# Block-sparse attention with a low-rank mixer on one core: casting transfers for half of the attention inputs

## The chip, the cores and the metric

The kernel runs on one core of a Trainium2 chip. The metric is the device time of one execution in microseconds (us), median of the runs. A core has a matrix engine (PE, with its weight loads shown as PEld), a vector engine (DVE), a scalar engine (ACT), GpSimd (POOL), and a queue engine (SP) that only issues transfers. Transfers are issued from SP's or POOL's queue (a few from ACT's) and are carried out by sixteen shared DMA engines. A *casting* transfer changes the type of the numbers as it writes them.

## The reference

Four batches, eight heads, 768 positions, 64 numbers a head. Attention with a mask by blocks of 32 positions (neighbours, first and last block, and three sampled blocks per row), then a mixer: a low-rank mix over positions, and two dense layers with a ReLU between them.

```python
scores = scale * np.matmul(q, k.transpose(0, 1, 3, 2))
scores = np.where(mask, scores, -1000000000.0)
attn = np.exp(scores - max) / (sum + 1e-09)
x = np.matmul(attn, v)                      # heads side by side: [4, 768, 512]
h = x.transpose(0, 2, 1) @ U @ V            # rank 32 over the positions
u = x + h.transpose(0, 2, 1)
out = u + np.maximum(u @ w_ch1, 0.0) @ w_ch2   # 512 -> 2048 -> 512
```

Inputs and outputs are 32-bit floats; the kernel computes its products from 16-bit floats.

## The kernel before

The heads are taken in pairs: 16 pairs, four to a batch (pairs 0 to 3 are batch 0, and so on). T = 6 tiles of 128 positions make up the 768. For a pair the work is: load q, k and v (384 KB each, as floats); cast each to a 16-bit tile; turn q and k so that a head's numbers lie along the partitions; score products on PE; exponentials on ACT; from pair 4 on, a product with the 0/1 mask on DVE (L1016); products with v on PE (L402); division by the row sum on DVE (L532, L539). When a batch's four pairs are done, its rows are mixed (`mix_all`, `mix_parts`), the 16-bit rows `xh` are turned into `uT` by four transposing transfers from SP (L611, `turn`), and the first dense layer starts from `uT` (L673, `w1`), its ReLU being on ACT (L685) or DVE (L687). The second layer follows (L748) with sums of weights and of hidden rows prepared on DVE (L709, L843), and its results are added to the float rows `xf` on DVE (L867, L891), which SP stores (L695, L893). While one batch's pairs run, PE fills up with the dense layers of the batch before. The last batch's layers stand alone at the end.

What the change and the prediction touch:

- `load_qk` (L145) and `load_v` (L158): for pair i, SP issues one transfer for each of q, k and v into a float tile (`ldpool`, two tiles of each kind in turn; rows of 1,536 bytes). Then `cast` (L136) has POOL copy it into the 16-bit tile: `stqld` and `stkld` for q and k (`stpool`, two of each in turn), and a slice of `vts[b % 2]` for v. From pair 6 on a cast is split into four of 128x192 (L142).
- `front(i)` (L373): for pairs 5 to 15, SP issues two transposing transfers (L375) from the 16-bit tiles of pair i to `qpl[i % 2]` and `kpl[i % 2]`. Each waits for the casts of pair i, and until PE is done with the scores of pair i - 2, which used the same target. The scores of these pairs are the products of L1001, in three groups a pair.
- `loads(i)` (L1024): calls `front(i + 1)`, and then the loads of pair i + 2, which `tc.issue_after` places behind that front in the order of issue.
- `load_w1` and `load_w2` (L351, L357): the dense layers' weights. They come by casting transfers that POOL issues straight into 16-bit tiles: four for w1 (128 rows of 8,192 bytes each), four for w2 (512 rows of 2,048 bytes each), the latter made by `hold` (L1036) when pair 4 begins.

The order of work on PE, DVE, ACT and SP is written out by hand: the words of `PLAN` (L436) are taken one after the other, and for instance `L.5` stands for `loads(6)`. POOL's order is not written out; the scheduler of the language sets it from what it reckons to be ready. All waits between engines follow from the tiles that an instruction reads and writes.

Of the kernel before, what the change touches and what calls it, by code (L numbers as in the profile page):

```python
# [13 lines left out]
FP16 = mybir.dt.float16  # L14
# [5 lines left out]
P = 128  # L20
# [3 lines left out]
def kernel(  # L24
# [14 lines left out]
    nc = tc.nc  # L39

    B, H, S, D = q.shape
    BLK = 32
    NB = S // BLK
    T = S // P
    HD = H * D
    HP = H // 2
# [32 lines left out]
    stpool = ctx.enter_context(tc.tile_pool(name="stpool", bufs=2))  # L79
# [34 lines left out]
    vts = [consts.tile([P, H, T, DV], FP16, name=f"vt{i}") for i in range(2)]  # L114
# [19 lines left out]
    sts = {}  # L134

    def cast(i, dst, ld):  # L136

        if i < HP + 2:
            return nc.gpsimd.tensor_copy(out=dst, in_=ld)
        for h in range(2):  # L140
            for ts in (slice(0, T // 2), slice(T // 2, T)):
                last = nc.gpsimd.tensor_copy(out=dst[:, h, ts], in_=ld[:, h, ts])  # L142
        return last

    def load_qk(i):  # L145
        b, hp = divmod(i, HP)
        last = None
        for src, nm in ((q, "qld"), (k, "kld")):
            ld = ldpool.tile([P, 2, T, D], FP32, tag="ld" + nm, name=nm)
            nc.sync.dma_start(  # L150
                out=ld,
                in_=src[b, 2 * hp : 2 * hp + 2].rearrange("h (p t) d -> p h t d", t=T),
            )
            sts[i, nm] = stpool.tile([P, T, 2, D], FP16, tag="st" + nm, name="st" + nm)
            last = cast(i, sts[i, nm].rearrange("p t h d -> p h t d"), ld)
        return last

    def load_v(i):  # L158
        b, hp = divmod(i, HP)
        ld = ldpool.tile([P, 2, T, D], FP32, tag="ldv", name="vld")  # L160
        nc.sync.dma_start(
            out=ld,
            in_=v[b, 2 * hp : 2 * hp + 2].rearrange("h (p t) d -> p h t d", t=T),
        )
        cast(i, vts[b % 2][:, 2 * hp : 2 * hp + 2, :, 0:D], ld)
# [67 lines left out]
    with tc.manual_schedule(  # L233
# [8 lines left out]
            out=sb[0:NB].rearrange("k z r w -> k (z r w)"),  # L242
            in_=sampled_blocks.bitcast(I32)
# [12 lines left out]
        for n in range(2):  # L256
# [3 lines left out]
            out=first, in_=nc.const_aps.tensor(1.0, [P, 1], FP32), func=AF.Exp  # L260
# [22 lines left out]
        def first_row(n, c, copy):  # L283
# [8 lines left out]
            out=neq[0:NB], in0=sb[0:NB, :, :, 0],  # L292
# [3 lines left out]
            out=a01[0:NB], in_=neq[0:NB], axis=mybir.AxisListType.X, op=ALU.min  # L296
        )
        nc.vector.scalar_tensor_tensor(
            out=bias[0:NB, :, 0:NB], in0=a01[0:NB, None].broadcast_to([NB, 2, NB]),
# [21 lines left out]
        for n in range(2):  # L321
            first_cast(1, n, nc.gpsimd.tensor_copy)
        nc.vector.memset(Ut, 0.0)
        load_v(0)
        load_qk(1)
        second_set()
        load_v(1)
        load_mix()

# [21 lines left out]
    def load_w1(cs):  # L351
        for cc in cs:
            nc.gpsimd.dma_start(
                out=w1t[:, cc, :], in_=moe_w_ch1[cc * P : (cc + 1) * P, :]
            )
# [13 lines left out]
    def plain(i):  # L369
        augs[i] = (qpl[i % 2], kpl[i % 2])  # L370
        return augs[i]

    def front(i):  # L373
        for nm, dst in zip(("qld", "kld"), plain(i)):
            last = nc.sync.dma_start_transpose(  # L375
                dst.rearrange("c (t p) -> c t p", t=T),
                sts[i, nm].rearrange("p t h d -> p (t h d)"),
            )
        return last
# [139 lines left out]
    class Pair:  # L519
# [6 lines left out]
        def divide(self, h, pav):  # L526
            head = 2 * self.hp + h
            if h == 0:
                self.xh = xpool.tile([P, T, P], FP16, tag="xh", name="xh", bufs=6)
                self.bt.xh[self.hp] = self.xh  # L530
            rcp = misc.tile([P, T], FP32, tag="rcp", name="rcp")
            nc.vector.reciprocal(out=rcp, in_=pav[:, :, D])  # L532
            xh = self.xh[:, :, h * D : (h + 1) * D]
            xf = self.bt.xf[:, :, head * D : (head + 1) * D]
            late = self.i >= HP + 2
            if late:
                then("y", lambda: nc.scalar.copy(out=xh, in_=xf))
            for dst in (xh, xf)[late:]:
                nc.vector.tensor_tensor(  # L539
                    out=dst, in0=pav[:, :, 0:D],  # L540
                    in1=rcp[:, :, None].broadcast_to([P, T, D]), op=ALU.mult,
                )
            if h and self.i == HP:
                loads(self.i + 1)
# [338 lines left out]
    def down_out(t, k):  # L883
# [17 lines left out]
        "x": lambda i, c: pairs[i].add_part(c), "d": lambda i, c: pairs[i].cast_part(c),  # L901
        "a": lambda b, c, jj, e: relus.pop((b, c, jj))("ba"[e]),
        "T": lambda i: pairs[i].turn(), "L": lambda i: loads(i + 1),
        "Z": lambda b, tau, u: store(b, 2 * tau + u),
        "S": pair_sum, "H": pair_down, "D": pair_out,
# [118 lines left out]
    def loads(i):  # L1024
        behind = ExitStack()
        if HP + 1 < i + 1 < NPAIR:
            behind.enter_context(tc.issue_after(front(i + 1).ins))
        if i + 2 < NPAIR:
            with behind:
                last = load_qk(i + 2)  # L1030
                load_v(i + 2)
            if i == 1:
                with tc.issue_after(last.ins):
                    load_w1(range(NCC))
# [10 lines left out]
    def begin(i):  # L1045
        if i and i % HP == 0:
            bts[i // HP] = Batch()
        pairs[i] = Pair(i, bts[i // HP])
        if i == HP:
            front(HP + 1)  # L1050
        elif i == HP + 2:
            for c in range(1, 4):
                nc.sync.dma_start(out=Vt[c * R : (c + 1) * R], in_=Vt[0:R])
        for m in {0: (0,), 1: (1, 2), 3: (3,), 4: (4,)}.get(i, ()):
            loads(m)
        if i == HP:
            hold(kpl[1])
# [105 lines left out]
```

## Time and profile before

| | |
|---|---|
| Median of 3 runs | 273.36 us (273.31 to 276.48) |
| Span of the profiled execution, first to last instruction | 271.1 us |
| Median over that span, for what lies around it | 2.3 us |
| Granted PE clock, mean over the span | 0.997 |
| POOL's casts of pairs 8 to 15 | 96, from 80.4 to 185.9 us |
| POOL's casts of pair 7 | end at 75.5 us |
| q transfer from SP, issue to landing, median | 3.5 us |
| k transfer, the same | 5.3 us |
| v transfer, the same | 4.6 us |
| Transposing transfer, issue to landing, median | 2.8 us |

Of the profiled execution only the span is given, not a time of its own; the table sets the median of the runs beside it. The profile's page gives each engine's busy time, and in 40 slices of the span (6.8 us each) the busy share in tenths, 9 being 90% or more. The view of waits sums the time that an engine stood idle before an instruction, by what ended it (total us, times, longest us). The view of a line gives its instructions' shortest, median and longest duration in ns and their first and last start in us. In the order of time a row is a start and a length in us.

### The profile page before, as it was taken

The page shows a single profiled execution, that of the slowest core. Times are in us where ns is not written, and L with a number is a line of the kernel's source. Part 1 is how long each engine was busy: PE and PEld are TensorE (multiplying, and loading weights), DVE is VectorE, ACT ScalarE, POOL GpSimd, SP SyncE. Part 2 cuts the span into 40 slices and gives each one's busy share as a digit, 9 for nine tenths or more (in the row PEclk, how much of TensorE's full clock was granted, in tenths as well). Part 3 has the DMA queues.
Part 4 walks back from the last instruction along what each step waited for, and adds up shares of the span by engine and source line. Part 5 has one row for each costly group of instructions (what it writes and reads, how often), then busy time and mean ns, then how long its engine had stood idle before and what let it go on. Part 6 is the DMA issues. An engine that isn't in the chain of part 4 may idle for free.

```text
span 271.1 us, 7373 instructions
## 1 busy us (share of the span) xinstructions
PE 261.9 (97%) x3008; PEld 182.1 (67%) x3008; DVE 235.3 (87%) x475; ACT 202.5 (75%) x264; POOL 84.7 (31%) x164
## 2 busy tenths in 40 slices
PE   7899999999999999999999999999999999999993
PEld 3577776555567778565666877565667788657882
DVE  5699988988999998868688997688998999999992
ACT  3889998897989666788888847788997943889100
POOL 4479104931628643035624660044000000000000
PEclk9999999999999999999999999999999999999998
DMA  5799997999974664872527356670200116300024
GB/s 161 239 305 316 199 210 173 225 131 198 155 222 67 201 204 91 278 217 59 178 45 190 64 212 117 221 208 16 46 0 2 41 41 142 134 0 0 22 78 136
DMA packets 49698, 37.58 MB, mean 139 GB/s; under 512 B 30528, under 2 KB 46816, under 8 KB 49664
## 3 DMA queue, kind: packets, MB, share of 16 engines
q1 hardware_dynamic: 46688, 32.67, 45.9%
q0 software_dynamic: 2688, 4.19, 10.9%
q8 instruction: 23, 0.38, 0.6%
q10 hardware_dynamic: 288, 0.24, 0.3%
q14 instruction: 11, 0.09, 0.1%
HBM read 27.67 MB, written 6.29 MB: 125 GB/s over the span
## 4 chain that ended last, share of the span: by engine, by line
PE 72%; DVE 17%; DMA 4%; ACT 2%; issue 1%; SPq 1%; POOL 0%; DVEq 0%; ACTq 0%
PE ps L748 28%; PE ps L673 20%; PE ps L402 9%; PE ps L1001 8%; DVE est L1016 5%; DMA qld<-in_q_dram 3%; PE ps L951 2%; DVE xf L867 2%; DVE xf L539 2%; DVE sums L843 1%; DVE res L709 1%; DMA vld<-in_v_dram 1%; ACT est L1010 1%; PE ps L970 1%; DVE sums L709 1%
## 5 line engine op out<-in xcount | busy, mean ns | idle before, releaser
L1010 ACT ACTIVATE est<-ps 128x1536 f16<-128x1536 f32 x72 | 100.6, 1450 | 18.9 <-PE ps L1001 18.9
L673 PE MATMUL ps<-uT,w1t 128*128 128x384 f16 x384 | 70.2, 326 | 0.2 <-DVE hid L687 0.2
L1016 DVE TENSOR_TENSOR est<-est,mask 128x1440 f16<-128x1440 f16 x72 | 65.5, 933 | 0.2
L673 PEld LDWEIGHTS <-w1t 128*128 128x128 f16 x384 | 35.6, 98 | 26.9 <-issue 7.0
L402 PEld LDWEIGHTS <-est 128*128 128x128 f16 x1152 | 40.2, 97 | 7.2 <-ACT hid L685 1.3
L402 PE MATMUL ps<-vt,est 128*128 128x65 f16 x1152 | 43.3, 193 | 0.1
L142 POOL CAST stqld<-qld 128x192 f16<-128x192 f32 x40 | 19.9, 540 | 73.2 <-DMA qld<-in_q_dram 36.0
L748 PEld LDWEIGHTS <-hid 128*128 128x128 f16 x360 | 34.3, 98 | 7.0 <-issue 1.9
L685 ACT ACTIVATE hid<-ps 128x384 f16<-128x384 f32 x63 | 29.7, 495 | 4.7 <-PE ps L673 4.3
L1001 PE MATMUL ps<-qpl,kpl 64*128 64x512 f16 (+1 forms) x288 | 31.6, 325 | 0.0
L748 PE MATMUL ps<-w2t,hid 128*128 128x256 f16 x240 | 31.3, 273 | 0.2 <-DVE xf L539 0.2
L867 DVE TENSOR_TENSOR xf<-xf,ps 128x256 f32<-128x256 f32 x63 | 25.0, 411 | 3.7 <-PE ps L748 3.3
L687 DVE TENSOR_SCALAR hid<-ps 128x384 f16<-128x384 f32 x33 | 18.2, 553 | 8.1 <-PE ps L673 7.5
L748 PEld LDWEIGHTS <-sums 128*128 128x128 f16 x216 | 20.3, 98 | 4.7 <-issue 1.1
L142 POOL CAST stkld<-kld 128x192 f16<-128x192 f32 x40 | 22.3, 597 | 2.5 <-DMA kld<-in_k_dram 2.5
L960 ACT ACTIVATE est<-ps 128x768 f16<-128x768 f32 x30 | 22.5, 813 | 0.6 <-PE ps L951 0.6
L1001 PEld LDWEIGHTS <-kpl 64*128 64x128 f16 x288 | 12.1, 94 | 14.3 <-issue 9.1
L748 PE MATMUL ps<-res,sums 128*128 128x256 f16 x144 | 19.4, 273 | 0.3 <-DVE xf L867 0.3
L622 ACT CAST xh<-xf 128x384 f16<-128x384 f32 x24 | 11.0, 510 | 10.4 <-DVE xf L618 10.4
L539 DVE TENSOR_TENSOR xf<-ps,rcp 128x384 f32<-128x384 f32 x32 | 17.7, 553 | 0.8
L142 POOL CAST vt<-vld 128x192 f16<-128x192 f32 x40 | 17.9, 487 | 0.0
L748 PE MATMUL ps<-res,hid 128*128 128x256 f16 x120 | 15.9, 273 | 0.0
(121 smaller groups left out, 341.5 us busy)
## 6 DMA issues: line engine op xcount, KB each, us to landing
vld<-in_v_dram SPq DMA_DIRECT2D x16, 384.0 KB, 4.6
qld<-in_q_dram SPq DMA_DIRECT2D x15, 384.0 KB, 3.5
kld<-in_k_dram SPq DMA_DIRECT2D x15, 384.0 KB, 5.5
out_dram<-xf SPq DMA_DIRECT2D x18, 256.0 KB, 2.2
w1t<-in_moe_w_ch_dram POOLq DMA_DIRECT2D x4, 512.0 KB, 8.2
w2t<-in_moe_w_ch_dram POOLq DMA_DIRECT2D x4, 512.0 KB, 10.4
out_dram<-xf SPq DMA_DIRECT2D x12, 128.0 KB, 1.7
qld<-in_q_dram SPq DMA_DIRECT2D x2, 192.0 KB
```

What stands on the lines that cost most here:

```text
L142: last = nc.gpsimd.tensor_copy(out=dst[:, h, ts], in_=ld[:, h, ts])
L402: nc.tensor.matmul(pav[:, sc, :], est[:, n, sc * P : (sc + 1) * P], vts[b % 2][:, 2 * hp + h, g, 0 : D + 1], start=(g == 0 and sc == 0), s ...
L539: nc.vector.tensor_tensor(out=dst, in0=pav[:, :, 0:D], in1=rcp[:, :, None].broadcast_to([P, T, D]), op=ALU.mult,)
L673: nc.tensor.matmul(pt, w1t[:, cc, jj * P : (jj + 1) * P], bts[b].uT[:, cc, c * HS : (c + 1) * HS], start=(cc == 0), stop=(cc == NCC - 1), ...
L685: nc.scalar.activation(out=dst, in_=pt, func=AF.Relu)
L687: nc.vector.tensor_scalar_max(out=dst, in0=pt, scalar1=0.0)
L748: nc.tensor.matmul(acc[key], lhsT, rhs, start=(first and i == 0), stop=(i == len(pairs_) - 1), skip_group_check=True,)
L867: nc.vector.tensor_add(out=x, in0=x, in1=acc[a, b, tau])
L960: lambda: nc.scalar.activation(out=dst, in_=ps, func=AF.Exp, scale=0.125),
L1001: nc.tensor.matmul(units[h][:, u * S + lo : u * S + hi], kT[drows[h], g * P : (g + 1) * P], qT[drows[h], lo:hi], start=True, stop=True, sk ...
L1010: nc.scalar.activation(out=both[h], in_=units[h].rearrange("p (g n) -> p g n", g=2), func=AF.Exp, scale=0.125,)
L1016: lambda: nc.vector.tensor_mul(out=masked(both[h]), in0=masked(both[h]), in1=masked(mask[:, 2 * j : 2 * j + 2, :]),),
```

## The change

For pairs 8 to 15 (batches 2 and 3) `load_qk` and `load_v` call a new function, `load_cast`, in which POOL issues casting transfers from the float inputs straight into the 16-bit tiles: one for each head of each of q, k and v, so six a pair, each of 768 rows of 64 numbers (256 bytes read, 128 written). The float tiles, SP's three transfers and POOL's twelve casts of such a pair are gone. The loads of these pairs are no longer placed behind the front of the pair before. Pairs 0 to 7 are unchanged.

```diff
+    DIRECT = 2 * HP
+
+    def load_cast(i, src, dst):
+
+        b, hp = divmod(i, HP)
+        for h in range(2):
+            nc.gpsimd.dma_start(
+                out=dst[:, h],
+                in_=src[b, 2 * hp + h].rearrange("(p t) d -> p t d", t=T),
+            )
+
     def load_qk(i):
         b, hp = divmod(i, HP)
         last = None
+        if i >= DIRECT:
+            for src, nm in ((q, "qld"), (k, "kld")):
+                sts[i, nm] = stpool.tile([P, T, 2, D], FP16, tag="st" + nm, name="st" + nm)
+                load_cast(i, src, sts[i, nm].rearrange("p t h d -> p h t d"))
+            return
...
     def load_v(i):
         b, hp = divmod(i, HP)
+        if i >= DIRECT:
+            load_cast(i, v, vts[b % 2][:, 2 * hp : 2 * hp + 2, :, 0:D])
+            return
...
         if HP + 1 < i + 1 < NPAIR:
-            behind.enter_context(tc.issue_after(front(i + 1).ins))
+            turned = front(i + 1)
+            if i + 2 < DIRECT:
+                behind.enter_context(tc.issue_after(turned.ins))
```

## The prediction

> **What bounds the kernel now.** I read the page's busy table and its 40 slices first, then the costliest groups and the waits, then the order of time of each queue that the change touches.
>
> ```profile
> PE 261.9 (97%) x3008; PEld 182.1 (67%) x3008; DVE 235.3 (87%) x475; ACT 202.5 (75%) x264; POOL 84.7 (31%) x164
> PE   7899999999999999999999999999999999999993
> POOL 4479104931628643035624660044000000000000
> DMA  5799997999974664872527356670200116300024
> ```
>
> PE is at 9 in every slice from the third to the last but one. POOL works only until two thirds of the span, and the sixteen DMA engines are about half used from slice 12 (81 us) to 28. POOL's casts of the last eight head pairs (8 to 15) lie between 80.4 and 185.9 us; that is where the change acts. So I asked what PE waits for from 76 to 190 us:
>
> ```profile
> PE ps L748 <- DVE xf L867: 0.3, 2, 0.2
> PE ps L653 <- DVE a L643: 0.2, 1, 0.2
> PE ps L748 <- DVE xf L539: 0.2, 1, 0.2
> ```
>
> In 114 us PE stands for 0.7 us, and never for a load. This is the most that a faster DVE or an earlier load can give back. The chain of waits puts DVE beside PE on the path (17%, against 72%), but there DVE and PE are both full: 19.76 and 19.52 us busy of the 20 us from 80 to 100.
>
> Then the product with the mask (L1016) on DVE, from 80 to 100 us with casts beside it, and from 186 to 215 us with none (columns: shortest, median, longest ns, first and last start):
>
> ```profile
> L1016 DVE TENSOR_TENSOR est<-est,mask x6: 894/984/1042, 83.7 to 92.0; 128x1440 f16<-128x1440 f16 x6
> L1016 DVE TENSOR_TENSOR est<-est,mask x15: 897/900/910, 185.9 to 214.8; 128x1440 f16<-128x1440 f16 x15
> ```
>
> A cast on POOL costs such a product up to 0.14 us. Last, what limits the new transfers: on SP, the last of the four turns of batch 1's tokens,
>
> ```profile
> 107.28 1.24 SPq L611 DMA_TRANSPOSE uT<-xh  x1
> ```
>
> PE's first use of it in the order of time,
>
> ```profile
> 110.18 0.82 PE L673 MATMUL ps<-uT,w1t 128*128 128x384 f16 x4
> ```
>
> and the issues that POOL makes already, with the DMA queues of the page (packets, MB, share of 16 engines):
>
> ```profile
> L359 POOL DMA_DIRECT2D w2t<-in_moe_w_ch_dram x4: 742/748/761, 48.1 to 55.8; - x4
> ```
>
> ```profile
> q1 hardware_dynamic: 46688, 32.67, 45.9%
> q0 software_dynamic: 2688, 4.19, 10.9%
> ```
>
> These turns land 2.7 to 2.8 us after their issue, so at 110.0 us, and PE comes for the result at 110.18. Batch 2 is alike: issue at 167.22, landing at 170.0, use at 170.25. Two spare gaps of 0.2 us are the tightest places near a DMA that I found.
>
> **The casts that go.** POOL loses 96 casts of 128x192 (0.35 us each when undisturbed, 0.34 to 1.06 in fact). None is on the path: front(8) on SP waits for its cast until 82.6 and 84.9 us, lands by 87.7, and the first scores of pair 8 run at 93.03; later pairs have more. What the casts cost is the collisions with DVE. I took each DVE operation from 80 to 190 us against the fast tenth of its own kind: the excess is 1.4 us (80 to 100), 1.4 (100 to 145), 0.9 (145 to 164) and 0.4 (164 to 190), 4.1 us together. PE can turn only its own 0.7 us of waiting into time. Bounds: 0 and 0.7 us; I take 0.5: the waits stand at 95, 99, 152 and 160 us, in or just behind stretches with casts.
>
> **The transfers that come.** Per pair 6 transfers from POOL take the place of 3 from SP. POOL's own time for one: w1's four transfers (128 rows each) took 0.54 to 0.67 us and w2's four (512 rows) 0.74 to 0.76. A new one has 768 rows; by the slope between those groups that is about 0.85 us, so 5.1 us a pair, against 4.0 to 7.6 us of casts now. Bounds: 0.54 us, and 1.1 if all of w2's 0.75 grew with the rows. The closest pairs follow each other after 12.3 us (first scores at 165.81 and 178.12), so POOL's time is hidden even at 1.1. DVE should not feel an issue: a mask product at 56.09, beside w2's issues (55.03 to 56.51), took 0.90 us, the undisturbed value.
>
> DMA time: the trace's packet records show, for transfers of POOL with a cast, 96 ns for 2,048 bytes read and 324 for 8,192 (medians), a straight line of 20 ns plus 0.037 ns a byte. A new packet (256 bytes read, 128 written) is then 30 ns. Bounds: 18 ns, the 256-byte packets of the transposes, and 96 ns, the cheapest cast packet seen. 768 packets on 16 engines are 48 each, 1.4 us a transfer and 8.6 us a pair, against 3.1 us now (48 packets of 65 ns). It is hidden while a load lands in time: the first needs come 4 us before a pair's first scores (turn 1.3 to issue, 2.8 to land).
>
> **What moves.** Loads of pair i+2 no longer stand on SP behind front(i+1); on POOL they wait only until front(i) has read the tile, as two tiles rotate. SP loses 1.5 us of issues a pair; front, the turns and the stores behind them come no later by it. On POOL the new issues are queued behind the casts of pair 7, which end at 75.5 us, or, if the scheduler puts them first, ahead of them from 56.7 on, when front(6) has landed. Pair 10's loads then follow front(8), pair 11's front(9) (after 88.8, when pair 7's last scores free the target), pair 12's front(10) (117.4), pair 15's front(13) (about 157). A POOL issue that waits holds only other loads behind it, and in one order pair 7's casts, whose front lands 3.5 us before its use. Value products now wait for the v transfer itself; they run after the pair's first scores, later than q and k are needed.
>
> **New collisions.** The turns of uT share the engines with loads. Before 100.8 us pair 11's loads should be nearly drained (issued at about 92 to 98, 8.6 us of data), and pair 12's wait until 117; pair 15's run from 155 to about 165 and meet the first two of four turns at 162.9. The slowest transpose of the trace, kpl's at 140.67 with loads issued right behind it, landed after 3.8 us and not 2.8: so the bound is 1.0 us at each of two places, less 0.2 us to spare, 1.6 us together; the lower bound is 0. I take 0.2, since the last turn, which counts, is clear of loads in both.
>
> Sum against this execution: span 271.1 - 0.5 + 0.2 = 270.8 us. The median of the three runs is 273.36, 2.3 us above the span for what lies around it; so I forecast 273.1 us. Own range: 273.4 - 0.7 to 273.4 + 1.6, 272.7 to 275.0.
>
> The trace holds no 128-byte write with a cast. Its 256-byte packets, the transposes', at 18 ns lie on the line of the larger plain ones (65 ns for 1,536 bytes, 84 for 2,048), so they show no surcharge for being small, and by them the sum stays 273.1. A page speaks against the change: the Trainium skill, "DMA: Bandwidth & Descriptors", section Specifications, has line rate begin at 512 bytes, with the engine reading, modifying and writing below that. It gives no price; by it the time would be that of rival 1.
>
> **Rivals.** (1) *The small packets make the DMA engines the bound.* Pair 15's q and k must land by about 199 us, and from 75.5 us on that leaves 123.5. Transposes (24 of 0.9 us) and stores (12 of 0.7) take 30, which leaves 93 us for 46 transfers: 2.0 us each, 42 ns a packet. Above that point it decides. At 50 ns the 46 take 110 us, 17 us too many: 290 us. At 96 ns it would be 119 us more. For it: 30 ns is stretched eightfold beyond the smallest cast packet seen, and small writes were not seen. Against it: the straight line, and the transposes' 18 ns. Chance 0.09.
>
> (2) *A wait moves into POOL's order.* POOL's order is the scheduler's: in the trace w2's issues stand between casts. If pair 8's six stood ahead of w2's last two, these would leave at 62 us and not at 55, and land some 8.6 us late, at 81 and not 72.7; DVE takes that part at 75.24. That is 6 us: 279 us. Against it: the w2 issues are made earlier in the program and are ready before front(6) lands. Chance 0.07.
>
> (3) *DVE's relief is worth all it measures*, 4.1 us: 269.3 us. For it: the chain is DVE's from 77 to 95 us. Against it: PE's idle time. Chance 0.04. That the transfers would not cast is no case here, as w1 and w2 are loaded so.
>
> **Chances.** Forecast 0.80, rivals 0.09, 0.07 and 0.04. About 2% (5.5 us) is what a measurement of this kernel can tell from no change. Faster by more needs over 5.5 us, which no case holds; 0.02 for what I missed. Slower takes (1) and most of (2): 0.14. Same: 0.84. The range takes the forecast's own with some room toward (2) and (3), and leaves out 0.18: 271.5 to 276.5.
>
> **What would show it.** Right: mask products at 0.90 us throughout from 80 to 190; POOL issues near 0.85 us; packets of 128 bytes near 30 ns; PE without a new wait at L673 after the turns. Wrong: PE waiting at L1001 for a front that waits for a load (rival 1), DVE at L709 waiting for w2 near 75 us (rival 2), transposes landing after 3.8 us or more, or POOL issues of 2 us.

## The result and the profile after

The changed kernel takes 273.55 us (median of 22 executions, 271.24 to 277.66) against 273.58 us of the kernel before (22 executions, 272.94 to 276.48). The ratio is 0.9939, with a 95% interval of 0.9911 to 0.9967; ratios leave out executions far above the fastest of their kernel, here the six highest of the change's 22 (275.76 us and up) and none of before's. The ratio of the medians of all executions is 1.000. The same kernel, measured once more beside the experiments, gave 274.08 us (272.14 to 278.75) and a ratio of 0.9994 (0.996 to 1.0028), or 1.002 by the medians. So the change is worth between nothing and six parts in a thousand, and the changed kernel reaches higher times than any of before's.

The first profile of the changed kernel is of an execution of 275.82 us (span 274.0 us), so the profile after is that of the second measurement: 272.87 us, span 271.1 us. Its page:

```profile
PE 262.0 (97%) x3008; PEld 182.4 (67%) x3008; DVE 233.9 (86%) x475; ACT 202.4 (75%) x264; POOL 74.9 (28%) x116
PE   7899999989999999999999999999999999999994
POOL 4488602792597670040404040000000000000000
DMA  6699999999999999894918696620200116400024
q0 software_dynamic: 40320, 8.92, 38.2%
q1 hardware_dynamic: 40160, 23.23, 35.8%
```

PE has the same sum, but not the same places: there is an 8 in the ninth slice (54 to 61 us), ahead of the stretch that the change acts on. DVE has lost 1.4 us. POOL is at 9 from 54 to 61 us and from 75 to 81, where it was at 3 and 2. In the queues, POOL's packets have gone from 2,688 to 40,320, and their share from 10.9% to 38.2%.

The mask products from 80 to 100 us (shortest, median, longest ns):

```profile
L1035 DVE TENSOR_TENSOR est<-est,mask x7: 895/901/910, 80.3 to 93.4; 128x1440 f16<-128x1440 f16 x7
```

None is longer than 0.91 us, where before the median was 0.98. What PE waited for from 78 to 215 us is down to one line:

```profile
PE ps L1020 <- DMA kpl<-stkld: 0.4, 1, 0.4
```

It is new: scores waiting for a turn of k, at 81 us. Ahead of that, from 50 to 78 us, PE has one wait, which explains the 8 in the ninth slice:

```profile
PE ps L1020 <- DVE hid L706: 0.9, 1, 0.9
```

It ends at 58.77 us. DVE comes late there because one mask product just before took twice its time, beside POOL's casts of pair 6:

```profile
56.34 1.91 DVE L1035 TENSOR_TENSOR est<-est,mask 128x1440 f16<-128x1440 f16 x1
56.86 1.89 POOL L142 CAST vt<-vld 128x192 f16<-128x192 f32 x4
```

The new issues on POOL, by tile:

```profile
L151 POOL DMA_DIRECT2D vt<-in_v_dram x16: 821/821/955, 15.7 to 100.5; - x16
L151 POOL DMA_DIRECT2D stqld<-in_q_dram x16: 821/821/821, 70.7 to 156.8; - x16
L151 POOL DMA_DIRECT2D stkld<-in_k_dram x16: 818/821/830, 78.2 to 158.4; - x16
```

An issue takes 0.821 us. The columns to look at are the first and last starts: q and k run from 70.7 to 158.4 us, as the prediction had it, but v begins at 15.7 us, for pairs whose scores come at 94 us and later.

To see where time went in and out of the executions, the start of each pair's first scores (L1001 before, L1020 after) is the best clock, since PE's order is written by hand and the same in all. The start of pair 4 differs by up to 2.8 us between the profiles; so stretches from pair 4 on are compared. Pairs 8 and 12, before (L1001) and after (L1020):

```profile
93.03 0.82 PE L1001 MATMUL ps<-qpl,kpl 64*128 64x512 f16 x8
165.81 0.82 PE L1001 MATMUL ps<-qpl,kpl 64*128 64x512 f16 x8
94.48 0.82 PE L1020 MATMUL ps<-qpl,kpl 64*128 64x512 f16 x8
166.17 0.82 PE L1020 MATMUL ps<-qpl,kpl 64*128 64x512 f16 x8
```

All stretches, in us:

| | pair 4 to 8 | pair 8 to 12 | pair 4 to the end |
|---|---|---|---|
| before | 49.63 | 72.78 | 227.74 |
| before, second profile | 50.30 | 72.50 | 228.14 |
| after | 50.83 | 71.69 | 227.45 |

The change gains 0.8 to 1.1 us between pairs 8 and 12, where the casts were, and loses 0.5 to 1.2 us between pairs 4 and 8, whose own loads are unchanged. PE's two new waits, 0.9 and 0.4 us, are as much as that loss. The loss isn't the same in every execution: in the first profile pair 4 to 8 takes 53.84 us, and PE waits 2.9 us for the turns of k of pairs 6 and 7. That is the question for the experiments: what costs time ahead of pair 8?

### The profile page after: what moved, and what is told of

It reads as the page before. It is cut to its first block, busy times and chain, and to the rows that moved or that the text cites. A ratio compares the mean times of both kernels' runs of the same rounds, so it can differ in the third digit from the quotient of the medians.

```text
span 274.0 us, 7321 instructions
## 1 busy us (share of the span) xinstructions
PE 263.5 (96%) x3008; PEld 183.4 (67%) x3008; DVE 232.8 (85%) x475; ACT 202.5 (74%) x264; POOL 74.8 (27%) x116
## 3 DMA queue, kind: packets, MB, share of 16 engines
q0 software_dynamic: 40320, 8.92, 38.4%
## 4 chain that ended last, share of the span: by engine, by line
PE 65%; DMA 11%; DVE 5%; POOL 3%; issue 1%; SPq 1%; ACT 0%; POOLq 0%
PE ps L767 31%; PE ps L692 17%; PE ps L1020 8%; PE ps L421 7%; DMA kld<-in_k_dram 5%; DMA vld<-in_v_dram 4%; DMA kpl<-stkld 3%; PE ps L672 1%; POOL stkld L142 1%; SPq L166 1%; POOL vt L142 1%; DVE est L1035 1%; POOL vt L139 1%; DVE xf L558 1%; DVE xf L910 1%
## 5 line engine op out<-in xcount | busy, mean ns | idle before, releaser
L692 PE MATMUL ps<-uT,w1t 128*128 128x384 f16 x384 | 70.2, 326 | 0.0
L1035 DVE TENSOR_TENSOR est<-est,mask 128x1440 f16<-128x1440 f16 x72 | 63.8, 907 | 0.6 <-ACT est L1029 0.2
L421 PEld LDWEIGHTS <-est 128*128 128x128 f16 x1152 | 41.3, 98 | 7.1 <-issue 2.7
L421 PE MATMUL ps<-vt,est 128*128 128x65 f16 x1152 | 44.2, 195 | 0.0
L1020 PE MATMUL ps<-qpl,kpl 64*128 64x512 f16 (+1 forms) x288 | 32.4, 330 | 3.0 <-DMA kpl<-stkld 2.9
L151 POOL DMA_DIRECT2D stqld<-in_q_dram x16 | 13.1, 821 | 51.7 <-DMA qpl<-stqld 51.7
L1020 PEld LDWEIGHTS <-kpl 64*128 64x128 f16 x288 | 12.5, 95 | 17.5 <-issue 9.4
L551 DVE RECIPROCAL rcp<-ps 128x6 f32<-128x6 f32 x32 | 6.2, 193 | 10.3 <-PE ps L421 10.1
L970 PE MATMUL ps<-res 128*128 128x384 f16 x60 | 14.0, 324 | 0.8 <-DVE res L300 0.5
```

The lines of the kernel that those rows point to most:

```text
L421: nc.tensor.matmul(pav[:, sc, :], est[:, n, sc * P : (sc + 1) * P], vts[b % 2][:, 2 * hp + h, g, 0 : D + 1], start=(g == 0 and sc == 0), s ...
L692: nc.tensor.matmul(pt, w1t[:, cc, jj * P : (jj + 1) * P], bts[b].uT[:, cc, c * HS : (c + 1) * HS], start=(cc == 0), stop=(cc == NCC - 1), ...
L970: nc.tensor.matmul(ps[:, c], kT[:, h, g * P : (g + 1) * P], qT[:, h, c * HS : (c + 1) * HS], start=True, stop=True,)
L1020: nc.tensor.matmul(units[h][:, u * S + lo : u * S + hi], kT[drows[h], g * P : (g + 1) * P], qT[drows[h], lo:hi], start=True, stop=True, sk ...
L1035: lambda: nc.vector.tensor_mul(out=masked(both[h]), in0=masked(both[h]), in1=masked(mask[:, 2 * j : 2 * j + 2, :]),),
```

## The experiments

The theory on trial: POOL's issues of v, which have no tile to wait for, go out early, and their small packets share the DMA engines with the loads and turns of pairs 5 to 7. Against it stood that the small packets cost time wherever they run, that the casts of pairs 8 to 15 never cost anything, and that what shows ahead of pair 8 is the scatter of any kernel. Each kernel is measured against the kernel before, in five rounds (the last one in three).

**The changed kernel again** (no edit), as the standard for the others.

> The changed kernel once more, for a profile of an execution that shows no dip of the granted clock. Theory A (small packets collide, DVE is relieved): its gain is DVE's relief, at most about 1.5 us, less what pair 7 pays because its turn of k shares the DMA engines with cast packets; in a good execution pair 7's first scores start under 1 us later than the 79.55 us of before, mask products are at 0.90 us from 80 to 190 us, ratio 0.990 to 0.997. Theory B (the relief is worth nothing, the difference is scatter of the loads of the first 80 us): pair 12's first scores lie no earlier, relative to pair 7's, than before (165.81 - 79.55 = 86.3 us).

Measured: 274.08 us, ratio 0.9994 (0.996 to 1.0028), outside theory A's range; pair 7 starts 1.5 us later than before's 79.55 us and not under 1. Theory B falls: pair 12 comes 85.1 us after pair 7, and not 86.3. POOL's order of time, rows of v and w2 alone:

```profile
15.75 0.95 POOL L151 DMA_DIRECT2D vt<-in_v_dram  x1
19.81 0.82 POOL L151 DMA_DIRECT2D vt<-in_v_dram  x1
29.39 1.65 POOL L151 DMA_DIRECT2D vt<-in_v_dram  x2
33.53 0.82 POOL L151 DMA_DIRECT2D vt<-in_v_dram  x1 [2.49 <-issue]
45.89 0.82 POOL L151 DMA_DIRECT2D vt<-in_v_dram  x1
58.70 1.48 POOL L378 DMA_DIRECT2D w2t<-in_moe_w_ch_dram  x2
60.16 2.45 POOL L151 DMA_DIRECT2D vt<-in_v_dram  x3
```

These are nine of v's sixteen, all eight of batch 2's among them. `vts` has two tiles by batch, and a pair's part of it is free once the value products of the pair eight before are done, so by 58 us nothing holds these issues back but POOL's own order. What they cost shows first at pair 5. The load of its q and POOL's cast of it, before and after:

```profile
33.99 0.59 SPq L150 DMA_DIRECT2D qld<-in_q_dram  x1
40.55 0.83 POOL L139 CAST stqld<-qld 128x768 f16<-128x768 f32 x1 [12.45 <-DMA qld<-in_q_dram]
37.13 0.52 SPq L166 DMA_DIRECT2D qld<-in_q_dram  x1
45.13 0.83 POOL L139 CAST stqld<-qld 128x768 f16<-128x768 f32 x1 [10.78 <-DMA qld<-in_q_dram]
```

From the issue to the cast it takes 8.0 us, and 8.1 in each of the two other profiles with v issued early (the first of the change, and v only); in the seven others it takes 5.4 to 6.7. In those 8 us the trace's packet records hold 2,234 packets of v, 5.2 us of all sixteen engines. Pair 5's turns, w2's issues behind them and pair 6's casts are late with it: w2's last issue starts 14.8 to 15.8 us after pair 4's first scores in these three profiles, and 12.3 to 13.0 in the seven others.

The last three issues of v run beside SP's loads of pair 7, issued from 60.27 to 61.46 us. SP's order of time, the turns of k of front(6) and front(7):

```profile
56.94 3.29 SPq L394 DMA_TRANSPOSE kpl<-stkld  x1
74.66 1.21 SPq L394 DMA_TRANSPOSE kpl<-stkld  x1
```

The first issue held SP for 3.3 us and not 1.2, and the loads of pair 7 behind it left later. No packet of v moved then: from 50 to 70 us the records hold none, but w2's, which are late. The second turn was used as soon as it had landed, at 81.07 us, 6.4 us after its start, against 2.8 us for a median transpose before. The three transfers of v from 60.16 us on landed only from 75.5 to 78.1 us, and the first two of pair 8's q at 79.1 and 80.8, so this turn shared the engines with both.

**v in order.** v's two transfers are queued on POOL behind the k transfers of their own pair.

```diff
...
-                load_cast(i, src, sts[i, nm].rearrange("p t h d -> p h t d"))
-            return
+                last = load_cast(i, src, sts[i, nm].rearrange("p t h d -> p h t d"))
+            return last
...
+                if i + 2 >= DIRECT:
+                    behind.enter_context(tc.issue_after(last.ins))
```

> The changed kernel, with the two v transfers of a pair queued on POOL behind the pair's k transfers, so that the scheduler can't issue them 10 to 60 us early. Theory A: fewer small packets beside w1, w2 and the loads of pairs 6 and 7; the turn of pair 7's k lands in under 5 us (8.2 in the first profile of the change), ratio 0.988 to 0.993, and less scatter than the change. Theory B: no different from the change, 0.994 within 0.002.

Measured: 272.71 us (271.55 to 273.79), ratio 0.9951 (0.9921 to 0.9981). Pair 4 to 8 takes 49.45 us, 8 to 12 71.69, 4 to the end 226.07. From 78 to 215 us the view of waits lists nothing for PE. Front(7)'s k turn is issued 5.1 us sooner than in the changed kernel (and 3.7 sooner than before's 73.26), though pair 4 began 2.3 us later in this execution:

```profile
69.58 1.21 SPq L395 DMA_TRANSPOSE kpl<-stkld  x1
```

The same transfers with the same packets, only later, cost nothing that shows. The loss lies in v's place in POOL's order. The ratio is above theory A's range and inside theory B's, which took the change to be worth 0.994; but the change, measured in the same rounds, came out at 0.9994. The two intervals still overlap a little. Over all executions the median is 273.90 us for the change (34) and 272.70 for v in order and held together (24).

**Held.** v in order, and in addition POOL's first instruction for each pair copies one element of the k target of the pair before, so that the whole group waits until that pair has been turned.

```diff
...
+                if nm == "qld":
+                    held = nc.gpsimd.tensor_copy(
+                        out=sts[i, nm][0:1, 0, 0, 0:1], in_=kpl[(i - 1) % 2][0:1, 0:1]
+                    )
+                    order.enter_context(tc.issue_after(held.ins))
...
```

> As v_in_order, and the first POOL instruction of each pair from 8 on copies one number out of the k turn of the pair before, so that no transfer of pair i starts before that turn has landed. Theory A: the turn of pair 7's k lands in 2.8 to 3.5 us as before the change, pair 7's scores are not late, ratio 0.988 to 0.993; it may give back up to 1 us where pair 10's loads now meet the turns of the tokens near 100 us. Theory B: 0.994 to 1.0.

Measured: 272.63 us (271.51 to 274.09), ratio 0.9947 (0.9914 to 0.9979); 49.37, 71.69 and 225.98 us. The ratio is in theory B's range, and it can't be told from v in order. With v held, the early q transfers (from 66.44 us on there, from 75.48 us on here) cost nothing that shows.

**No casts.** The kernel before without the loads and casts of pairs 8 to 15; SP fills their q and k tiles from a tile on the chip, and v keeps what it held.

```diff
+        if i >= 2 * HP:
+            for src, nm in ((q, "qld"), (k, "kld")):
+                sts[i, nm] = stpool.tile([P, T, 2, D], FP16, tag="st" + nm, name="st" + nm)
+                nc.sync.dma_start(
+                    out=sts[i, nm].rearrange("p t h d -> p (t h d)"),
+                    in_=Vt.rearrange("p t q -> p (t q)"),
+                )
+            return
...
+        if i >= 2 * HP:
+            return
```

> The kernel before, without loads and casts of pairs 8 to 15: SP copies 1,536 bytes a partition from another 16-bit tile into each q and k tile, and v is not loaded, so batches 2 and 3 are computed from other numbers. It is the ceiling of what the casts of these pairs cost. Theory A: 0.75 to 1.5 us less than before, ratio 0.994 to 0.997 from PE's waiting alone, down to 0.988 if the full 4.1 us of DVE excess counts. Theory B: 1.000.

Measured: 271.69 us (271.07 to 274.56), ratio 0.9927 (0.9887 to 0.9967); 49.55, 71.69 and 226.18 us. The ratio is a little below the range from PE's waiting alone (0.994 to 0.997) and far from 0.988. This is what the loads and casts of these pairs are worth together. From pair 8 to 12 it takes 71.69 us, the same to a hundredth as the change, v in order and held, which have the 128-byte packets and no casts there. So in that stretch the 128-byte packets cost PE nothing, and the casts cost it 0.8 to 1.1 us.

**v only** and **q, k only.** The kernel before with `load_cast` for one part; the other keeps its float tiles and casts.

```diff
...
     def load_v(i):
+        if i >= DIRECT:
+            load_cast(i, v, vts[b % 2][:, 2 * hp : 2 * hp + 2, :, 0:D])
+            return
```

> The kernel before, with the change for v alone: q and k of pairs 8 to 15 by SP and casts as before, v by casting transfers in whatever order the scheduler gives them. Theory A (the change's cost is v's transfers, issued early): it has that cost and at most a third of the casts' relief, so 0.5 to 3 us slower than before, ratio 1.002 to 1.011, pair 7 late by 1 us or more against pair 4. Theory C (the cost comes from the transfers as such, wherever they stand): the cost is a third of the change's, ratio 0.998 to 1.001.

Measured: 273.84 us (272.42 to 279.39), ratio 0.9998 (0.9961 to 1.0035): no gain, and a highest time above any of before's. The ratio lies in theory C's range and not in A's. The profile is of an execution of 278.47 us (span 276.7), the second longest of the 12, so its lengths are only hints: pair 7 comes 39.8 us after pair 4, against 36.2 and 35.9 before, late as theory A had it, and pair 8 to 12 takes 73.06 us, as if the casts of q and k that are left kept the relief away. Its order and waits can be read: v is issued from 16.93 us on, as in the changed kernel, and from 60 to 100 us PE waits for pair 6's k turn:

```profile
PE ps L1015 <- DMA kpl<-stkld: 2.2, 1, 2.2
PE ps L416 <- DVE xf L553: 0.5, 1, 0.5
```

So v's part alone, with q and k as before, brings the early issues and a wait of the same kind. All three profiles with v issued early have a wait of PE for a turn of k (0.4, 2.9 and 2.2 us), and none of the seven others has one. How much of it an execution of ordinary length has, these profiles can't tell.

```diff
...
     def load_qk(i):
+        if i >= DIRECT:
+            for src, nm in ((q, "qld"), (k, "kld")):
+                sts[i, nm] = stpool.tile([P, T, 2, D], FP16, tag="st" + nm, name="st" + nm)
+                load_cast(i, src, sts[i, nm].rearrange("p t h d -> p h t d"))
+            return
```

> The kernel before, with the change for q and k alone; v by SP and casts as before. Theory A: no early transfers, 64 of 96 casts gone, ratio 0.995 to 0.998, pair 7 not later against pair 4 than before; from pair 8's first scores to the end 0.5 to 1.1 us shorter than before. Theory C: two thirds of the change's cost, pair 7 late by 0.8 us or more, ratio 0.998 to 1.003.

Measured: 275.02 us (273.39 to 276.81), ratio 1.0009 (0.9975 to 1.0044). The ratio is again in theory C's range; but pair 7 isn't late (36.1 us after pair 4), as theory A had it, and theory C can't stand beside v in order and held, which have all the transfers and gain. The profile is of the longest execution, 276.81 us. In it pair 4 to 8 takes 50.07 us, within the two values of before, so q and k lose nothing there. But 8 to 12 takes 73.07 us: none of the relief, though two casts of three are gone. The third that is left, v's, now stands where DVE is full:

```profile
78.53 3.04 POOL L142 CAST vt<-vld 128x192 f16<-128x192 f32 x4
86.95 2.80 POOL L142 CAST vt<-vld 128x192 f16<-128x192 f32 x4
```

Four casts take 3.0 us there and 1.2 us alone, and PE waits behind DVE from 78 to 110 us:

```profile
PE ps L418 <- DVE xf L555: 0.7, 1, 0.7
PE ps L669 <- DVE a L659: 0.6, 1, 0.6
PE ps L764 <- DVE xf L883: 0.2, 1, 0.2
```

In this one profile, where a cast stands matters more than how many there are. The wait of 0.6 us at 102 us follows a sum on DVE (L725, at 99.10) that took 1.63 us and not 0.68, beside the cast of 98.97.

**The kernel before again** (no edit).

> The kernel before, once more, as a measure of what two equal kernels differ by here, and for a second profile: ratio 0.997 to 1.003. From PE's last product to the end it took 4.5 us in the first profile and 4.1 in four others; if that is scatter, this one may show either, and if the change does it, 4.5 again.

Measured: 273.59 us (273.19 to 276.29), ratio 0.9993 (0.9958 to 1.0028). By its interval, a ratio above 0.996 can't be told from that of two equal kernels here. Its profile gave the second row of before in the table.

**Half rows.** v in order, with every transfer cut in two, so twice as many packets, of 64 bytes each.

```diff
...
-            last = nc.gpsimd.dma_start(
-                out=dst[:, h],
-                in_=src[b, 2 * hp + h].rearrange("(p t) d -> p t d", t=T),
-            )
+            for c in range(2):
+                ds = slice(c * D // 2, (c + 1) * D // 2)
+                last = nc.gpsimd.dma_start(
+                    out=dst[:, h, :, ds],
+                    in_=src[b, 2 * hp + h, :, ds].rearrange("(p t) d -> p t d", t=T),
+                )
```

> The change with v in order and every transfer cut in two, rows of 32 numbers (128 bytes read, 64 written): 12 transfers of 768 packets a pair. By the straight line a packet takes 25 ns, so 14.3 us of all engines a pair and 115 us in all. The budget of the first rival was 93 us from 75 us on: by it pair 15 is about 15 to 20 us late, ratio 1.05 to 1.08. If the budget was too strict, because loads run ahead and stages are uneven, 0.995 to 1.02. POOL's issues, 0.82 us each, take 9.8 us a pair and should not bind.

Measured: 279.92 us (277.93 to 283.61), ratio 1.0179 (1.0105 to 1.0253). POOL's queue on the page, and what PE waits for from 60 to 240 us:

```profile
q0 software_dynamic: 77952, 8.92, 58.1%
```

```profile
PE ps L695 <- DMA uT<-xh: 5.9, 3, 3.0
PE ps L695 <- DVE hid L709: 0.3, 1, 0.3
```

A row of 128 bytes read and 64 written takes 27 ns (median; the prediction's line gives 25), so a pair's transfers take 12 x 48 x 27 ns = 15.6 us of all engines, in place of 9.2. PE waits for no load even so. It waits 5.9 us for the turns of the tokens: of three turns whose landing the trace tells, two took 5.1 and 6.2 us from issue to landing, and one 2.8 as before. The products behind such a wait ran slower as well (L695 takes 72.9 us in all and 70.2 before, at a granted clock of 0.93 from 100 to 125 us); the two together, 8.6 us, are near the 8.5 us that pair 8 to the end lost against before (186.6 and 178.1 us), though the 0.8 to 1.1 us of the casts should have come off. The median lost 6.4 us, well short of the 1.05 to 1.08 that the first rival's budget gave, and inside the range for a budget that was too strict.

## Why the prediction was right, and where not

The forecast of 273.1 us was 0.5 us off the first measurement and 1.0 us off the second, and the range held both. That its sum, -0.5 + 0.2, came out so near is luck: the relief was larger by 0.3 to 0.6 us, and a loss of 0.5 to 1.2 us that was put at nothing took it back. The sum's base was off as well: in each measurement of the change the time of an execution is 1.7 to 1.8 us above its span, not 2.3. The 2.3 set a median beside a profiled execution that was shorter than it, by 271.1 + 1.8 = 272.9 us. That moves the level and not the forecast change.

- **DVE's relief: mis-sized.** "PE can turn only its own 0.7 us of waiting into time" was a step that failed. The relief is 0.8 to 1.1 us, 71.69 against 72.50 and 72.78 us, in five profiles alike (both of the change, v in order, held, no casts). The list of waits counts from a matmul's modelled end. Taken from the start of one matmul to the start of the next, beyond what its columns take, before has hand-overs of 0.35, 0.33, 0.34 and 0.38 us at 94.9, 99.0, 151.3 and 159.9 us, where a plain one is 0.10. All four are gone after; 4 x 0.25 us is 1.0 us. That most of DVE's 4.1 us of collisions gives PE nothing was right (rival 3 fell).
- **DVE and POOL: right.** "DVE should not feel an issue": with 0.82-us issues beside them the products from 80 to 100 us take 0.90 us; beside casts there they took up to 1.04. The Trainium skill, "SBUF — State Buffer", section "Who interferes with whom", says that a DVE instruction with two inputs from SBUF contends with a GpSimd instruction that reads SBUF. The traces agree for the casts. Most products beside casts lose up to 0.14 us, but two operations in the ten profiles lost 1.0 us: the mask product of 1.91 us at 56.34 in the profile after, and the sum of 1.63 us at 99.10 in q, k only.
- **POOL's issue: right.** 0.821 us measured, 0.85 taken.
- **Packets: right.** 128 bytes take 32 ns (median; 31 to 32 from the shortest to nine in ten), 30 taken; rival 1 needed 42. The Trainium skill, "DMA: Bandwidth & Descriptors", section Specifications, has the engine read, modify and write below 512 bytes; 27 ns for 64 bytes written and 32 for 128, against 25 and 30 by the line from larger packets, leave 2 ns for that, and the time of rival 1 did not come. Rival 1's budget was wrong in its place too: with 69% more engine time a pair (15.6 us and 9.2), it is the token turns that PE waits for, and no load.
- **What moves: wrong for v.** "on POOL they wait only until front(i) has read the tile, as two tiles rotate" holds for q and k. v goes into a part of a batch's tile that is free after the value products of the pair eight before. Its issues were costed at nothing, on the ground that value products come later than q and k are needed; being early is what cost: 0.5 to 1.2 us between pairs 4 and 8 against before, and 1.3 to 1.5 us against v in order, held and no casts (50.83 us and 49.37 to 49.55). The prediction asked whether new transfers would come late, and looked for collisions only at the turns of the tokens, from 100.8 us on. Two of its signs of being wrong did show, at pair 7 and small: PE waits 0.4 us for a front whose loads are late, and that turn took 6.4 us and not under 3.8.
- **New collisions at the token turns: not there.** 0.2 us was taken; in the profile after PE waits for none of the 14 turns, and the three whose landing the trace tells took 2.8 us. The place had little to spare, as half rows show, but not at this load.
- **w2 and rival 2: no.** w2's last issues left from 58.70 us on, 3.7 us later than before, and DVE waited for none of it. Rival 2's heading, a wait that moves into POOL's order, was near what happened, with v in w2's place.

Shown: the relief and its size (no casts, v in order, held); that the loss goes when v's place in the order is changed and nothing else (v in order); and that pair 5's q comes later wherever v is issued early (three profiles against seven). Only argued: the way from there to each of PE's waits. Of the 1.3 us in the profile after, 0.4 are a turn's, and 0.9 come from one stretched mask product; that v's place brings that collision about, by making pair 6's casts late, is not shown. Left open: the size of the loss in an ordinary execution; the kernel before itself has executions of 275 to 276.5 us, which v in order, held and no casts, with 36 executions between them, never have, and none of those was profiled; and the end of the kernel from PE's last product on takes 4.24 us in both profiles of before and 3.85 in most of the others, half rows with 4.31 among the exceptions, so it isn't the casts.

The best version is v in order, or held: 0.9951 and 0.9947. The changed kernel's first measurement is as good, its second is not; in v in order and held the highest of 24 executions is 274.09 us, in the changed kernel of 34 it is 278.75.

## What to carry to other kernels

When loads move to a queue whose order a scheduler sets, ask of each what still holds it back: one with nothing to wait for goes out at once, and takes its share of the DMA engines from whatever is needed then. Give it a place in the order by hand. Profile more than one execution, and look at every new wait, also ahead of the place that the change acts on. Bound what a relieved engine can give by gaps from start to start on the bounding engine, not by its list of waits alone, and look at where the remaining collisions will stand, not only at how many are taken away.

## What the runs showed that was not expected

- A transposing transfer that shares the engines with many 128-byte packets came late: 6.4 us from issue to the use that waited for it, against 2.8; with 64-byte packets, up to 6.2 us to landing.
- A DVE operation beside casts on POOL mostly lost 0.14 us at the most, but two lost 1.0 us: one took 1.91 us and not 0.90, and PE waited 0.9 us behind it; the other took 1.63 us and not 0.68.
- A 64-byte write costs nearly as much as one of 128 bytes (27 and 32 ns), so cutting the rows of the transfers in half raised their time on the engines by 69%.
- In half rows PE paid twice for a wait: 5.9 us of waiting came with 2.7 us of slower products, at a granted clock of 0.93 from 100 to 125 us.
